# A convolution with a routed feed-forward network: a later group's placing put behind the first slot's turn, fewer parts ahead, and three more groups convolved by parts

## Chip, cores and metric

The kernel runs on one core of one Trainium2 chip. The metric is the device time of one execution in microseconds, taken as the median of several runs. Profiles come from one further execution, recorded by the hardware profiler. Engine names are those of the profile: PE is TensorE (PEld its weight loads), DVE is VectorE, ACT is ScalarE, POOL is GpSimd, and SP is SyncE, which here only issues DMAs (its queue is SPq).

## The reference

Two stages. First a causal depthwise convolution over the sequence: 8 sequences of 3584 tokens with 192 channels, 7 taps per head, 8 heads of 24 channels, the taps of a head made by a softmax. Then a top-1 routed network on the 28672 tokens that come out:

```python
w = softmax(weight)                                   # (8 heads, 7 taps)
x = causal_conv(x, w).reshape(28672, 192)             # float32
logits = x @ w_gate + modality_bias[modality_id]      # (28672, 8)
e_idx = argmax(logits, 1); gate = softmax(logits)[e_idx]
out[t] = gate[t] * (relu(x[t] @ w1[e]) @ w2[e])       # e = e_idx[t]; w1 192x1024, w2 1024x192
```

Everything is float32 in and out.

## The kernel before, in words

**Groups.** The convolution and the routing work on 19 groups of tokens (`QUADS_OF_GROUP`, 1, 1, 2, 2, 2 and then 4 quads each; a quad is four tiles of 112 tokens). A group is loaded (`load`, L246), convolved head by head on PE (`convolve`, L266) into a PSUM bank of 8 heads in turn, and copied from there into a buffer `y` in SBUF by ACT for two heads of three and by DVE for the third (L281, L283). There are four `y` buffers; a group of four quads takes two of them, and writes them again only when the scatters of the group that had them have landed. Then come, quad by quad, a transposition on DVE (`turn`, L300), a split for the gate (`part_turned`, L303), the gate's product on PE (`gate`, L320), the logits (L327), and for the whole group `choose` (L334, softmax and argmax on DVE, an exponential on ACT) and `place` (L364, the row of each token in its expert's list, on DVE, from two small PE products). `send` scatters the rows to DRAM by indirect DMAs on POOL (L212).

**Two ways to convolve.** Groups below `WHOLE_X` keep x as float32 in one tile and need one float32 matmul per head with the float32 band (the trace shows it as two MATMUL instructions). The others split x into a rounded half `xh` (ACT, L100) and the remainder `xl` (DVE, L101), quad by quad in `part` (L257), and take three matmuls in the reduced format F32R per head. Their quads are loaded into a ring of three buffers, `xr_0` to `xr_2`, so the fourth quad's load waits for the split of the first. The float32 band lies in the buffer of `xr_0` (L157) as long as a group below `WHOLE_X` is still to be convolved.

**Slots.** The network runs in slots: one expert, 512 rows (chunk 0) or 1024 rows, read back from the scattered lists. Ten chunks of groups feed the slots; chunk 0 is groups 0 to 4 and feeds four slots of two passes of 256 rows. A slot loads w1 and w2 (L623 to L628) and splits them into halves (`split`, L666), brings its rows by DMA (`bring`, L634: `near`, `far`, `tags`), and turns them pass by pass (`turn`, L676: two DVE transpositions, ACT casts, DVE remainders). A pass has four steps: `first` (ten matmuls into `hps`, a ReLU on ACT to `hh`, its remainder `hl` on DVE) and, two steps later, `second` (eight matmuls into two banks `po`), and at the pass's end `put` (an ACT and a DVE operation for each bank, then a scatter to the output).

**Order.** The program is written as generators. `all_groups` (L449) yields after each small part of a group's work; `advance` (L769) runs the next part. `through("groups", 0)` runs the groups of chunk 0; it ends just behind the first head of group 5. Then `start(0)` (L885) brings slot 0, runs `AHEAD` more parts, and writes slot 0's turn. With `AHEAD` 26 these are the rest of group 5, its choice included, and heads 0 and 1 of group 6. After that `run` (L837) writes step by step, and `due` (L795) says how many parts are to have been written by each step: a straight line between marks, the first at `head + AHEAD`. A compiler pass then orders each engine's instructions from its own estimate of when they become ready, so that later work can move ahead of earlier work, with one exception: the ACT instructions written inside `run` keep the order in which they are written (`manual_schedule`, L902). `tc.issue_after(ins)` puts an instruction behind `ins` on the engine of `ins`. All engines execute their queue in order.

Of the kernel before, what the change touches and what calls it, by code (L numbers as in the profile page):

```python
# [14 lines left out]
ALU = mybir.AluOpType  # L15
AX = mybir.AxisListType
PSUM = bass.MemoryType.PSUM

P = 128
MB = 112  # L20
HALO = 16
QUADS_OF_GROUP = (1, 1, 2, 2, 2) + (4,) * 14
WHOLE_X = 10
WHOLE_Y = 5
HEAD_BANKS = dict(turn=1, logit=2, place=2)
ORDERED = {mybir.EngineType.Activation}
# [2 lines left out]
WAIT = 3  # L29
OUTS = 4  # L30
PIN = 18
AHEAD = 26
T = 256
GROUPS_OF_CHUNK = (5, 2, 2, 2, 2, 2, 2, 2, 0, 0)
SLOTS_OF_CHUNK = (4, 3, 3, 4, 3, 4, 3, 3, 3)
# [8 lines left out]
def conv_then_routed_ffn(ctx, tc, x, weight, modality, w_gate, mod_bias, w1, w2, out):  # L44
    nc = tc.nc
    NB, S, D = x.shape
# [8 lines left out]
    NF = FF // P  # L55
    NJ = T // P
# [54 lines left out]
    def warm(n):  # L111
# [9 lines left out]
        out=tri, in_=ones, compare_op=ALU.is_gt, fill=0.0, base=0,  # L121
# [10 lines left out]
    carry = const.tile([MB, E], F32, name="carry0")  # L132
# [91 lines left out]
    class Group:  # L224
# [109 lines left out]
        def choose(self):  # L334

            n = self.tiles
            lg = self.lg

            def per_tile(ap):
                return ap.unsqueeze(2).broadcast_to([MB, n, E])  # L340

            top = rt.tile([MB, NT], F32, name="top")[:, 0:n]
            nc.vector.tensor_reduce(out=top, in_=lg, axis=AX.X, op=ALU.max)
            ex = rt.tile([MB, NT, E], F32, name="ex", bufs=1)[:, 0:n]
            nc.vector.tensor_tensor(out=ex, in0=lg, in1=per_tile(top), op=ALU.subtract)
            nc.scalar.activation(out=ex, in_=ex, func=AF.Exp)
            self.oh = rt.tile([MB, NT, E], BF16, name="oh")[:, 0:n]
            rk = rt.tile([MB, NT, E], F32, name="rk", bufs=1)[:, 0:n]
            nc.vector.tensor_tensor(out=rk, in0=lg, in1=per_tile(top), op=ALU.is_equal)
            nc.vector.tensor_tensor(out=rk, in0=rk, in1=ramp.unsqueeze(1).broadcast_to([MB, n, E]), op=ALU.mult)  # L350
            first = rt.tile([MB, NT], F32, name="first")[:, 0:n]
            nc.vector.tensor_reduce(out=first, in_=rk, axis=AX.X, op=ALU.max)
            nc.vector.tensor_tensor(out=self.oh, in0=rk, in1=per_tile(first), op=ALU.is_equal)
            den = rt.tile([MB, NT], F32, name="den")[:, 0:n]
            nc.vector.tensor_reduce(out=den, in_=ex, axis=AX.X, op=ALU.add)
            nc.vector.tensor_scalar(out=den, in0=den, scalar1=1e-9, scalar2=None, op0=ALU.add)
            for i, y in enumerate(self.ys):
                nc.vector.reciprocal(out=y[0:MB, 0:self.nb, 0], in_=den[:, i * self.nb:(i + 1) * self.nb])
                with tc.issue_after(state["scatter"]) if "scatter" in state else nullcontext():
                    nc.gpsimd.iota(y.bitcast(I32)[0:MB, 0:self.nb, 1], pattern=[[S, self.nb]],  # L360
                                   base=self.b0 * S + (self.block + i) * MB + MB - 1,
                                   channel_multiplier=-1)

        def place(self):  # L364

            n = self.tiles
            oh = self.oh
            rp = self.bank("place", [MB, 2, n, E], F32, "rp")
            ohf = oh.rearrange("p t e -> p (t e)")
            nc.tensor.matmul(rp[:, 0].rearrange("p t e -> p (t e)"), tri, ohf, start=True, stop=True)  # L370
            nc.tensor.matmul(rp[:, 1].rearrange("p t e -> p (t e)"), ones, ohf, start=True, stop=True)
            ad = rt.tile([MB, E * NT], F32, name="ad", tag="ex", bufs=1)[:, 0:E * n].rearrange("p (e t) -> p e t", e=E)
            nc.vector.tensor_copy(out=ad[:, :, 0], in_=state["carry"])
            nc.vector.tensor_copy(out=ad[:, :, 1:n], in_=rp[:, 1, 0:n - 1, :].rearrange("p t e -> p e t"))
            base = rt.tile([MB, E * NT], F32, name="base", bufs=1)[:, 0:E * n].rearrange("p (e t) -> p e t", e=E)
            nc.vector.tensor_tensor_scan(
                out=base.rearrange("p e t -> p (e t)"), data0=keep[n].rearrange("p e t -> p (e t)"),
                data1=ad.rearrange("p e t -> p (e t)"), initial=0.0, op0=ALU.mult, op1=ALU.add)
            after = rt.tile([MB, E], F32, name="carry", bufs=4)
            nc.vector.tensor_tensor(out=after, in0=rp[:, 1, n - 1, :], in1=base[:, :, n - 1], op=ALU.add)  # L380
            pos = rt.tile([MB, NT, E], F32, name="pos", tag="rk", bufs=1)[:, 0:n]
            nc.vector.tensor_tensor(out=pos, in0=rp[:, 0], in1=base.rearrange("p e t -> p t e"), op=ALU.add)
            nc.vector.tensor_tensor(out=pos, in0=pos, in1=oh, op=ALU.mult)
            row = rt.tile([MB, NT], F32, name="row")[:, 0:n]
            nc.vector.tensor_reduce(out=row, in_=pos, axis=AX.X, op=ALU.add)
            self.idx = rt.tile([MB, NT], I32, name="idx", bufs=6)[:, 0:n]
            nc.vector.tensor_copy(out=self.idx, in_=row)
            state["carry"] = after
            state["placed"] += 1
            if state["placed"] == sum(GROUPS_OF_CHUNK[:self.chunk + 1]):  # L390
                state["end", self.chunk] = after
# [19 lines left out]

    def body(cur, after):

        if after:
            for q in range(min(3, after.quads)):
                after.load(q)
        for h in range(H):
            cur.convolve(h)
            yield
        cur.bias_of()  # L420
        gates = []
        ready, step_of = [], 1 if cur.whole_y else 2
        for t in range(cur.quads + 2):
            if t < cur.quads:
                cur.turn(t)
                yield
            if t == 0 and after and after.whole_x and after.quads > 3:
                after.load(3)
            if ready and ready[0][1] < t:
                t0, _, terms = ready.pop(0)  # L430
                gates.append((t0, cur.gate(terms)))
            yield
            if t < cur.quads:
                terms = cur.part_turned(t)
                if (t + 1) % step_of == 0 or t + 1 == cur.quads:
                    ready.append((4 * (t // step_of * step_of), t, terms))
            yield
            while gates:
                cur.logits(*gates.pop(0))
        cur.choose()  # L440
        yield
        if after and not after.whole_x:
            for q in range(after.quads):
                after.part(q)
                if q == 0 and after.quads > 3:
                    after.load(3)
                yield
# [33 lines left out]
    state, tables = {}, {}  # L481
# [129 lines left out]
    class Slot:  # L611


        def __init__(self, i, chunk, ent):
            self.i, self.h, self.passes, self.rows, self.ends, self.tags = i, {}, plan[chunk][2] // T, {}, {}, {}
            self.chunk, self.ent, load = chunk, ent, nc.sync
            with tc.issue_after(state["load"]) if "load" in state else nullcontext():
                e = load.value_load(ent[:, 1:2], min_val=0, max_val=E - 1)
                new = load.value_load(ent[:, 2:3], min_val=0, max_val=1)
            w1e = w1[bass.ds(e, 1), :, :].rearrange("e p n -> (e p) n")  # L620
            w2e = w2[bass.ds(e, 1), :, :].rearrange("e (c p) d -> p (e c) d", p=P)
            only = dict(cond=new, cond_hint=False)
            load.dma_start(out=raw1[i % 2][:, 0, :], in_=w1e[0:P, :], **only)  # L623
            for r in range(2):
                state["load"] = load.dma_start(out=raw1[i % 2][r * DB:(r + 1) * DB, 1, :], in_=w1e[P:D, :], **only).ins
# [50 lines left out]
        def turn(self, k):  # L676
            lot, k0 = divmod(k, LOT)
            tp = ring(sp, 2, [P, NJ + 1, P], F32, "tp")
            with tc.issue_after(state["o"]) if "o" in state else nullcontext():
                nc.vector.transpose(out=tp[:, 0:NJ].rearrange("p j (s t) -> p (j s) t", t=Q),  # L680
                                    in_=self.rows[lot][:, k0 * T // Q:(k0 + 1) * T // Q])
# [8 lines left out]
            for hi, lo, raw in pieces:  # L690
                turned = nc.vector.tensor_tensor(out=lo, in0=raw, in1=f(hi), op=ALU.subtract).ins  # L691
            self.h["x", k] = [z.rearrange("p j s -> p (j s)") for z in (xh, xl, xs)]
            self.h["tag", k] = self.tags[lot][:, k0 * NJ:(k0 + 1) * NJ]
            state["vector"] = turned

        def first(self, k, fp):
            wa = w1b[self.i % 2]
# [13 lines left out]
        def second(self, k, fp):  # L711
            wb = w2b[self.i % 2]
            hh, hl = self.h.pop((k, fp))
            if fp == 0:
                self.po = [ring(ps_g2, 2, [P, 2 * D], F32, "po") for _ in range(NJ)]
            for u in range(2):
                c = 2 * fp + u
                for j, po in enumerate(self.po):
                    js = slice(j * P, (j + 1) * P)

                    def by_hi():
                        nc.tensor.matmul(po, hh[:, u, js], wb[:, c, :], start=c == 0, stop=c == NF - 1,  # L722
                                         skip_group_check=True)

                    def by_lo():
                        nc.tensor.matmul(po[:, 0:D], hl[:, u, js], wb[:, c, 0:D], start=False, stop=False,  # L726
                                         skip_group_check=True)

                    for product in (by_lo, by_hi) if c == NF - 1 else (by_hi, by_lo):
                        product()  # L730
            if fp == NF // 2 - 1:
                self.put(self.h.pop(("tag", k)))

# [201 lines left out]
```

## Time and profile before

| | |
|---|---|
| median of 3 runs | 1276.77 us (1275.79 to 1277.69) |
| the profiled execution | 1274.14 us, its span 1272.4 us |
| PE busy in the span | 1221.3 us (96%) |
| DVE, ACT, POOL busy | 1001.7, 736.9, 519.2 us |
| granted TensorE clock, mean | 0.987 |

A row of the timeline gives the start in us from the span's start, the duration, the engine, the line of the code, the operation, what is written and read, a count of merged instructions, and in brackets the idle time of the engine just before and what ended it. A row of a table by windows gives for each engine the busy time in that stretch and the number of instructions, then the granted TensorE clock as a share, the DMA share and GB/s. A row of the waits gives the total, the number and the longest. A row of the chain of work gives start, duration and what the last-ending chain passed through. Groups of instructions show busy time and the mean ns of one, then idle time before them.

### The profile page before, as it was taken

The page shows a single profiled execution, that of the slowest core. Times are in us where ns is not written, and L with a number is a line of the kernel's source. Part 1 is how long each engine was busy: PE and PEld are TensorE (multiplying, and loading weights), DVE is VectorE, ACT ScalarE, POOL GpSimd, SP SyncE. Part 2 cuts the span into 40 slices and gives each one's busy share as a digit, 9 for nine tenths or more (in the row PEclk, how much of TensorE's full clock was granted, in tenths as well). Part 3 has the DMA queues.
Part 4 walks back from the last instruction along what each step waited for, and adds up shares of the span by engine and source line. Part 5 has one row for each costly group of instructions (what it writes and reads, how often), then busy time and mean ns, then how long its engine had stood idle before and what let it go on. Part 6 is the DMA issues. An engine that isn't in the chain of part 4 may idle for free.

```text
span 1272.4 us, 28546 instructions
## 1 busy us (share of the span) xinstructions
PE 1221.3 (96%) x9106; PEld 1187.7 (93%) x9106; DVE 1001.7 (79%) x2545; ACT 736.9 (58%) x1644; POOL 519.2 (41%) x574
## 2 busy tenths in 40 slices
PE   8559999999999999999999999999999999999996
PEld 6438899999999999999999999999999999999996
DVE  6559988887888778877888788877876676687895
ACT  2226565566666556656665666556555555566774
POOL 5745763625353532624454442613526122121221
PEclk9869999999999999999999999999999999999999
DMA  6567475435453445424355445424424135494440
GB/s 180 158 164 174 125 196 106 108 83 134 100 145 79 98 95 120 133 44 111 63 133 147 110 103 119 114 56 103 101 48 132 37 77 109 104 248 105 91 101 18
DMA packets 314836, 142.24 MB, mean 112 GB/s; under 512 B 229042, under 2 KB 301355, under 8 KB 314676
## 3 DMA queue, kind: packets, MB, share of 16 engines
q1 hardware_dynamic: 289060, 94.97, 35.4%
q0 software_dynamic: 23232, 44.30, 11.0%
q8 instruction: 73, 1.20, 0.4%
q10 hardware_dynamic: 2384, 1.06, 0.3%
q14 instruction: 87, 0.71, 0.2%
HBM read 118.16 MB, written 51.82 MB: 134 GB/s over the span
## 4 chain that ended last, share of the span: by engine, by line
PE 77%; DVE 7%; issue 4%; DMA 4%; POOL 3%; SPq 2%; ACT 2%; DVEq 0%; POOLq 0%; ACTq 0%
PE hps L704 36%; PE po L722 23%; PE po L726 11%; PE cv L276 5%; PE gt L320 3%; POOL routed_rows L212 2%; DVE hl L708 2%; SPq L653 2%; DVE w1b L101 1%; DMA raw<-in_moe_w_dram 1%; DMA routed_rows<-y,idx 1%; DVE w2b L101 1%; DMA near<-routed_rows 1%; ACT lowp L738 0%; DVE sxs L691 0%
## 5 line engine op out<-in xcount | busy, mean ns | idle before, releaser
L722 PE MATMUL po<-w2b,hh 128*128 128x384 f32 x1824 | 556.2, 355 | 3.6 <-DVE o L740 3.4
L704 PE MATMUL hps<-sxh,w1b 128*128 128x256 f32 x1824 | 484.7, 288 | 2.7 <-DVE hl L708 1.3
L741 POOL DMA_INDIRECT out_dram<-o,tags x228 | 233.6, 1024 | 555.8 <-DVE o L740 492.2
L707 ACT ACTIVATE hh<-hps 128x512 fp32r<-128x512 f32 x456 | 273.1, 599 | 314.4 <-PE hps L704 309.1
L708 DVE SCALAR_TENSOR_TENSOR hl<-hps,hh 128x512 fp32r<-128x512 f32 x456 | 311.2, 685 | 178.0 <-ACT hh L707 175.5
L726 PE MATMUL po<-w2b,hl 128*128 128x192 f32 x1824 | 442.6, 253 | 0.0
L704 PE MATMUL hps<-sxs,w1b 128*128 128x256 f32 x1824 | 363.3, 281 | 0.5 <-DVE sxs L691 0.5
L704 PEld LDWEIGHTS hps<-sxh,w1b 128*128 128x128 f32 x1824 | 343.9, 189 | 12.7 <-DVE hl L708 7.9
L722 PEld LDWEIGHTS po<-w2b,hh 128*128 128x128 f32 x1824 | 344.1, 189 | 5.4 <-DVE o L740 4.8
L726 PEld LDWEIGHTS po<-w2b,hl 128*128 128x128 f32 x1824 | 345.7, 190 | 0.0
L212 POOL DMA_INDIRECT routed_rows<-y,idx x256 | 253.7, 991 | 145.4 <-issue 114.2
L704 PEld LDWEIGHTS hps<-sxs,w1b 128*128 128x128 f32 x1824 | 279.6, 189 | 0.9 <-DVE sxs L691 0.7
L704 PE MATMUL hps<-sxl,w1b 128*128 128x256 f32 x912 | 256.1, 281 | 0.6 <-DVE sxl L691 0.6
L704 PEld LDWEIGHTS hps<-sxl,w1b 128*128 128x128 f32 x912 | 172.5, 189 | 3.2 <-DVE sxl L691 0.8
L101 DVE TENSOR_TENSOR w1b<-raw,w1b 128x512 fp32r<-128x512 f32 x152 | 101.1, 675 | 6.6 <-ACT w1b L100 6.1
L738 ACT ACTIVATE lowp<-po,tags 128x192 f32<-128x192 f32 x228 | 83.7, 418 | 31.8 <-PE po L722 31.3
L281 ACT COPY y<-cv 112x192 f32<-112x192 f32 (+1 forms) x198 | 53.4, 319 | 75.5 <-PE cv L276 54.6
L100 ACT CAST w1b<-raw 128x512 fp32r<-128x512 f32 x152 | 92.4, 620 | 0.8
L101 DVE TENSOR_TENSOR w2b<-raw,w2b 128x384 fp32r<-128x384 f32 x152 | 80.9, 542 | 10.3 <-ACT w2b L100 10.0
L740 DVE SCALAR_TENSOR_TENSOR o<-po,tags,lowp 128x192 f32<-128x192 f32 x228 | 84.9, 411 | 4.8 <-ACT lowp L738 2.5
L689 ACT CAST sxs<-tp 64x128 fp32r<-64x128 f32 x228 | 67.9, 298 | 32.6 <-DVE tp L682 29.8
L100 ACT CAST w2b<-raw 128x384 fp32r<-128x384 f32 x152 | 76.1, 512 | 1.0
(133 smaller groups left out, 1032.0 us busy)
## 6 DMA issues: line engine op xcount, KB each, us to landing
raw<-in_moe_w_dram SPq DMA_DIRECT2D x38, 768.0 KB
raw<-in_moe_w_dram SPq DMA_DIRECT2D x38, 512.0 KB
raw<-in_moe_w_dram SPq DMA_DIRECT2D x76, 256.0 KB
xr<-in_x_dram SPq DMA_DIRECT2D x36, 384.0 KB
near<-routed_rows SPq DMA_DIRECT2D x212, 64.0 KB
x<-in_x_dram SPq DMA_DIRECT2D x26, 384.0 KB
far<-routed_rows SPq DMA_DIRECT2D x456, 16.0 KB
routed_rows<-filler SPq DMA_DIRECT2D x8, 776.0 KB
```

The source lines that it names most:

```text
L100: nc.scalar.copy(out=hi, in_=raw)
L101: return nc.vector.tensor_tensor(out=lo, in0=raw, in1=f(hi), op=ALU.subtract).ins
L212: state["scatter"] = nc.gpsimd.indirect_dma_start(out=scr, out_offset=bass.IndirectOffsetOnAxis(ap=idx, axis=0), in_=src, in_offset=None,).ins
L689: nc.scalar.copy(out=hi, in_=raw)
L704: nc.tensor.matmul(hps[:, u, :], wa[:, c, fs], mv[z], start=n == 0, stop=n == len(terms) - 1)
L707: nc.scalar.activation(out=hh, in_=hps, func=AF.Relu)
L708: turn_behind(nc.vector.scalar_tensor_tensor(out=hl, in0=hps, scalar=0.0, in1=f(hh), op0=ALU.max, op1=ALU.subtract))
L722: nc.tensor.matmul(po, hh[:, u, js], wb[:, c, :], start=c == 0, stop=c == NF - 1, skip_group_check=True)
L726: nc.tensor.matmul(po[:, 0:D], hl[:, u, js], wb[:, c, 0:D], start=False, stop=False, skip_group_check=True)
L738: nc.scalar.activation(out=lowp, in_=po[:, D:2 * D], func=AF.Copy, scale=gate)
L740: turn_behind(nc.vector.scalar_tensor_tensor(out=o, in0=po[:, 0:D], scalar=gate, in1=lowp, op0=ALU.mult, op1=ALU.add))
L741: st = nc.gpsimd.indirect_dma_start(out=out, out_offset=bass.IndirectOffsetOnAxis(ap=tag.bitcast(I32)[:, j, 1:2], axis=0), in_=o, in_offse ...
```

## The change

Seven edits, all in the program's text:

1. `WHOLE_X` 10 to 7: groups 7, 8 and 9 are convolved by parts. `parts_of` then counts four more parts for each of groups 6, 7 and 8, at whose end the next group is split.
2. `AHEAD` 26 to 24: heads 0 and 1 of group 6 are no longer written before slot 0's turn, but in `run`.
3. `state["first"]` is the last DVE instruction of slot 0's turn. `choose` puts its first DVE instruction behind it, and so does `place`, where that turn has been written already: the placing of group 5 and everything of later groups.
4. `band_free` in `body`: where the next group is the first by parts (now group 7), its quads are loaded after the current group's eight heads, not before.
5. The weight loads of slots 0 and 1 are no longer conditional.
6. `second`: in a pass's last step the four pairs of matmuls go by bank (both for the first bank, then both for the second) and not in alternation.
7. The marks of `due` move with the counts of parts.

```diff
-WHOLE_X = 10
+WHOLE_X = 7
-AHEAD = 26
+AHEAD = 24
...
 def choose(self):
...
-            nc.vector.tensor_reduce(out=top, in_=lg, axis=AX.X, op=ALU.max)
+            with tc.issue_after(state["first"]) if "first" in state else nullcontext():
+                nc.vector.tensor_reduce(out=top, in_=lg, axis=AX.X, op=ALU.max)
...
 def place(self):
...
-            nc.vector.tensor_copy(out=ad[:, :, 0], in_=state["carry"])
+            with tc.issue_after(state["first"]) if "first" in state else nullcontext():
+                nc.vector.tensor_copy(out=ad[:, :, 0], in_=state["carry"])
...
 def body(cur, after):
-        if after:
+        band_free = after and cur.whole_x and not after.whole_x
+        if after and not band_free:
             for q in range(min(3, after.quads)):
                 after.load(q)
         for h in range(H):
             cur.convolve(h)
             yield
+        if band_free:
+            for q in range(min(3, after.quads)):
+                after.load(q)
...
 class Slot: __init__
-            only = dict(cond=new, cond_hint=False)
+            only = dict(cond=new, cond_hint=False) if i > 1 else {}
...
 class Slot: turn
             state["vector"] = turned
+            state.setdefault("first", turned)
...
 class Slot: second
-            for u in range(2):
-                c = 2 * fp + u
-                for j, po in enumerate(self.po):
-                    js = slice(j * P, (j + 1) * P)
+            at = [(u, j) for u in range(2) for j in range(NJ)]
+            if fp == NF // 2 - 1:
+                at = sorted(at, key=lambda uj: uj[1])
+            for u, j in at:
+                c, po = 2 * fp + u, self.po[j]
+                js = slice(j * P, (j + 1) * P)
...
```

The products themselves (`by_hi`, `by_lo`) and their order within a pair are unchanged.

More of the change, by code (lines that the diff above doesn't have):

```diff
@@ L715, in second, with by_hi, by_lo @@
                 self.po = [ring(ps_g2, 2, [P, 2 * D], F32, "po") for _ in range(NJ)]
-            for u in range(2):
-                c = 2 * fp + u
-                for j, po in enumerate(self.po):
-                    js = slice(j * P, (j + 1) * P)
[L721 to L730, printed above, removed]
+            at = [(u, j) for u in range(2) for j in range(NJ)]
[4 more added lines that the diff above has]
+                js = slice(j * P, (j + 1) * P)
+                def by_hi():
+                    nc.tensor.matmul(po, hh[:, u, js], wb[:, c, :], start=c == 0, stop=c == NF - 1,
+                                     skip_group_check=True)
+                def by_lo():
+                    nc.tensor.matmul(po[:, 0:D], hl[:, u, js], wb[:, c, 0:D], start=False, stop=False,
+                                     skip_group_check=True)
+                for product in (by_lo, by_hi) if c == NF - 1 else (by_hi, by_lo):
+                    product()
             if fp == NF // 2 - 1:
```

## The prediction

> **What bounds the kernel now.** I read the page first, then busy time by windows, then who PE waited for, then the timeline of the opening. The page gives the frame:
>
> ```profile
> span 1272.4 us, 28546 instructions
> PE 1221.3 (96%) x9106; PEld 1187.7 (93%) x9106; DVE 1001.7 (79%) x2545; ACT 736.9 (58%) x1644; POOL 519.2 (41%) x574
> ```
>
> PE is idle for 51.1 us in all (1272.4 - 1221.3). The windows say where, and how DVE stands there:
>
> ```profile
> 60.00:80.00 20.00, 7.73 (x25) 5.55 (x26) 7.27 (x32) 5.55 (x11) 9.06 (x14) 0.57 0.43 106
> 80.00:100.00 20.00, 13.39 (x73) 9.65 (x72) 15.78 (x47) 7.53 (x23) 11.24 (x11) 0.91 0.89 230
> 110.00:120.00 10.00, 8.68 (x67) 8.24 (x66) 9.77 (x22) 6.43 (x13) 3.53 (x7) 1.00 0.63 124
> 120.00:130.00 10.00, 9.13 (x60) 7.76 (x59) 8.70 (x29) 6.04 (x18) 2.07 (x3) 1.00 0.89 222
> 130.00:140.00 10.00, 10.00 (x67) 8.86 (x67) 8.86 (x28) 6.45 (x18) 6.87 (x7) 1.00 0.78 216
> 140.00:150.00 10.00, 8.61 (x65) 7.95 (x64) 9.96 (x30) 5.78 (x12) 8.07 (x7) 1.00 0.22 65
> 150.00:160.00 10.00, 8.69 (x66) 8.25 (x66) 9.77 (x32) 5.16 (x11) 8.32 (x9) 1.00 0.37 114
> 400.00:500.00 100.00, 99.85 (x766) 99.32 (x765) 80.80 (x183) 61.35 (x134) 35.91 (x41) 1.00 0.44 100
> ```
>
> Three stages. From 60 to 100 us PE is idle for 18.9 of 40 us: the passage from the convolution's head to the first slot. From 110 to 160 us DVE is the fuller engine (47.06 of 50 us against PE's 45.11). From 400 us PE is 99.85% busy, so there only work taken from PE counts. What PE waited for:
>
> ```profile
> PE cv L276 <- ACT y L281: 14.4, 4, 6.9
> PE gt L320 <- ACT gx L100: 8.8, 3, 5.9
> PE po L722 <- DVE o L740: 3.4, 5, 0.9
> ```
>
> The opening, from the timeline:
>
> ```profile
> 61.94 0.54 ACT L281 COPY y<-cv 112x192 f32<-112x192 f32 x2 [3.84 <-DMA routed_rows<-y,idx]
> 62.37 0.84 ACT L100 CAST gx<-turned 128x768 fp32r<-128x768 f32 x1
> 75.78 0.54 ACT L281 COPY y<-cv 112x192 f32<-112x192 f32 x2 [7.16 <-DMA routed_rows<-y,idx]
> 75.88 1.96 SPq L653 DMA_DIRECT2D near<-routed_rows  x4
> 76.15 2.90 PE L276 MATMUL cv<-x,band 128*112 128x384 f32 x4 [6.90 <-ACT y L281]
> 78.03 4.39 SPq L653 DMA_DIRECT2D far<-routed_rows  x8
> 78.27 2.27 PE L320 MATMUL gt<-gx,wg_parts 128*128 128x256 f32 x11
> 80.58 0.45 DVE L327 STREAM_TRANSPOSE lt<-gt 128x256 f32<-128x256 f32 x1 [9.66 <-PE gt L320]
> 83.29 0.39 SPq L628 DMA_DIRECT2D raw<-in_moe_w_dram  x1
> 85.79 0.16 DVE L373 COPY ad<-carry 112x8 f32<-112x8 f32 x1
> 88.50 0.17 DVE L387 CAST idx<-row 112x16 int32<-112x16 f32 x1
> 88.68 0.45 DVE L680 STREAM_TRANSPOSE tp<-near 128x256 f32<-128x256 f32 x1
> 90.57 0.30 DVE L682 STREAM_TRANSPOSE tp<-far 128x128 f32<-128x128 f32 x1
> 91.90 0.50 PE L704 MATMUL hps<-sxs,w1b 128*128 128x256 f32 x2 [0.45 <-DVE sxs L691]
> 93.65 1.76 ACT L100 CAST w2b<-raw 128x384 fp32r<-128x384 f32 x4
> 95.73 0.61 ACT L707 ACTIVATE hh<-hps 128x512 fp32r<-128x512 f32 x1
> ```
>
> Read it from the end. The second ReLU (95.73) follows the splits of w2 (93.65), they follow the first ReLU, and that the products from 91.90. Those came late because DVE turned the rows at 88.68, directly behind group 5's choice and placing (85.79 to 88.67 is the placing). Choice and placing were late because group 5's logits (80.58) came late: PE had four convolution matmuls of group 6 ahead of the gate's products, and these waited for PSUM banks that ACT's copies of heads 0 and 1 of group 6 were to free (61.94 and 75.78). Those copies waited, 3.84 and 7.16 us long, for scatters that still read the `y` buffers. The same copies held up group 5's own cast (62.37).
>
> **The change, part by part.** *Fewer parts ahead.* Heads 0 and 1 of group 6 now belong to the part in which ACT keeps the written order, behind the first ReLU. So the four copies leave the opening: group 5's cast and gate no longer stand behind them, and with the gate, logits and choice come before the rows of slot 0 arrive. *Placing behind the turn.* The 2.88 us (85.79 to 88.67) go behind slot 0's turn. What queues behind the delayed placing on DVE: the first remainder `hl`; and behind its result, group 5's sixteen scatters on POOL, for which nobody waits before chunk 1's slots. The cover is the wait for w2 that follows; without it this would cost up to 2.9 us.
>
> What is late next in the opening is data, worked out with landings from the chain of work (the convolution rows serve further down; the x6 row is from the chain's stretch of 288 to 304 us):
>
> ```profile
> 1.65 4.70 DMA x<-in_x_dram
> 103.87 1.48 DMA far<-routed_rows
> 161.21 1.29 PE cv L276 x4
> 290.45 1.04 PE cv L276 x6
> 405.80 2.68 DMA near<-routed_rows
> 1233.00 4.05 DMA raw<-in_moe_w_dram
> ```
>
> `near`: the last issue ends at 77.84, landed 80.5 (+2.68). `far` for the first pass is the first four of eight issues, to 80.2, landed 81.7 (+1.48). From the turn of `far` to the products that need it took 1.33 us (90.57 to 91.90). So these products could run at 83.0 instead of 91.90, if DVE is free. But then w2 is late: issued until 83.68, landed 87.7 at the earliest (+4.05). ACT then splits it (1.76), makes the four copies of heads 0 and 1, now in its way (2 x 0.54), and comes to the second ReLU at 90.5 instead of 95.73: 5.2 us earlier. I take off 1 us, since w2's 768 KB are the larger of the weight loads, and 1.3 us for two convolutions of group 6 that PE did in idle time and now does behind the slot's start (x4 in 1.29 us is two of them). Opening: **-2.9 us**, bounds 0 (the passage is late by something else) and -5.2.
>
> The clock speaks against part of this. After 6.90 us of idling the x4 convolutions at 76.15 took 2.90 us; warm they took 1.29 (161.21). The first slot's products now come after a longer pause, so they will start at that slower rate. I set 0 for it: they lie between 83 and 88 us, where ACT waits for w2 anyway. The Trainium skill, page "TensorE: Matmul & The Clock Gate", Part 1, says that after a window of about 3.4 us without work the array gets half its clock, until about 3.4 us of work have passed; by that rule, without my cover, some 1.7 us (an estimate from that page) would be added and the sum below be -2.5. The rate of the two rows agrees with it.
>
> *Groups 7 to 9 by parts.* Taken from PE: 24 convolutions at 0.645 us (1.29 / 2) become three matmuls each at 0.52 (1.04 / 2). **-3.0 us**, in full only where PE is the bound; bounds 0 and -3.0. Added, per quad:
>
> ```profile
> L101 DVE TENSOR_TENSOR xl<-xr,xh 128x768 fp32r<-128x768 f32 x36 | 33.9, 941 | 0.2
> L100 ACT CAST xh<-xr 128x768 fp32r<-128x768 f32 x36 | 29.8, 829 | 0.7 <-DMA xr<-in_x_dram 0.5
> ```
>
> and, in the timeline, group 10's first and last cast:
>
> ```profile
> 281.20 0.83 ACT L100 CAST xh<-xr 128x768 fp32r<-128x768 f32 x1
> 287.56 0.82 ACT L100 CAST xh<-xr 128x768 fp32r<-128x768 f32 x1
> ```
>
> Twelve quads: 11.3 us on DVE, 9.9 on ACT. ACT has room (6 of 10 us busy in the windows). For DVE it depends on the place. Group 9's quads and group 8's last fall where DVE has a fifth to spare, as at 400 us: 0. Group 7's split (3.8 us) follows group 6's choice, in the full stretch from 110 to 160 us, which has 2.9 us of DVE to spare (50 - 47.06). Between 0 (all of it fits) and 3.8 (nothing does) I take **+2.2**, nearer to the upper end, because the windows with room are not those beside the full ones; for group 8 the same bounds, and 0.
>
> *Halves in turn.* The first bank is finished one pair of matmuls earlier.
>
> ```profile
> L722 PE MATMUL po<-w2b,hh 128*128 128x384 f32 x1824 | 556.2, 355 | 3.6 <-DVE o L740 3.4
> ```
>
> A pair is about 0.3 us of PE (556.2 / 1824; its small partner mostly overlaps). PE waited five times, 3.4 us together, for `o`. At 0.3 us each at most 1.5; nothing at least. I take **-0.5**.
>
> *Later loads, unconditional weights, moved marks.* Group 7's loads leave SP's queue behind w2, so slot 1's weights go out sooner; PE did not wait for them: 0. Without the condition SP issues slot 0's w1 some tenths sooner, but ACT took it up at 76 us behind its own wait, and rows set the opening: 0. The first mark lies 21 steps ahead (32 steps of chunk 0 less `LEAD`), with groups 5 to 7 written by then: 25 + 29 + 29 - 24 = 59 parts, before 75 - 26 = 49. Group 6's placing stays at about step 11 (32 parts at that rate, before 26): 0.
>
> Sum: -2.9 - 3.0 + 2.2 - 0.5 = **-4.2 us**. On the profiled execution's 1274.14 us this gives 1269.9; the median of the runs lies 2.6 us above that execution, so I put 1276.77 - 4.2 = **1272.6 us**. About 0.2% (2.55 us) is what a measurement of this kernel can tell from no change.
>
> **Rivals.** *The vector engine overflows (slower).* At 59 parts in 21 steps (2.81 a step) the splits of groups 7 and 8 are pressed together. The rows at 281.20 and 287.56 show four casts spread over 6.4 us where 54 parts were due in 48 steps (1.13); at the new rate they come within 6.4 x 1.13 / 2.81 = 2.6 us. The fourth quad's load can only go after the first remainder (0.94) and needs some 4.7 us to land (first row of the chain), 5.6 together. ACT keeps its order, so it stands for up to 3.0 us per group, and the ReLUs behind it. With 7.6 us of remainders without room and one such wait, and without the gain of the convolutions of groups 7 and 8: -2.9 - 1.0 - 0.5 + 7.6 + 3.0 = +6.2, **1283.0 us**. For it: 9.96 and 9.77 of 10 us. Against: from 120 to 140 us DVE has 2.4 us left. It turns the forecast to slower once the two groups cost more than 2.2 + 4.2 + 2.55 = 9.0 us together.
>
> *The opening stays (no change).* The compiler's own order may put other DVE work ahead of the turn (group 6's head copies that wait for the same scatters), or w2 and the moved convolutions eat the 5.2 us. Then -3.0 + 2.2 - 0.5 = -1.3, **1275.5 us**. For it: before, that order put the placing ahead of the turn although it was written behind. Against: the copies on ACT do go.
>
> *All of it counts (faster still).* The opening gives 5.2 and the splits find room: -5.2 - 3.0 - 0.5 = -8.7, **1268.1 us**.
>
> **How the numbers follow.** Forecast 0.48, opening stays 0.24, overflow 0.18, all counts 0.10. The forecast's own range is 1269 to 1275 (the opening within 1.1 us of its value, group 7's split between 0 and 3.8); about a tenth of it reaches over the line of -2.55. So faster 0.10 + 0.46 = 0.56, same 0.24 + 0.02 = 0.26, slower 0.18. The range from 1266.5 to 1280 leaves out the upper half of the overflow and little at the lower end.
>
> **What would show it.** In the changed profile: no ACT copy at 62 and 76 us that waits for scatters; group 5's logits before 75 us; the turn of `near` at 80 to 82 us and the placing behind it; the ReLU of the second step at 90 to 92 us; 48 L276 matmuls on the float32 band of 128x384 fewer and 72 by parts more; PE's wait for `o` under 3 us. I am wrong if the turn comes after 86 us, if ACT or SP waits over 2 us for an `xr` load between 110 and 180 us, or if PE's idle time there grows by more than 5 us.

## The result, and the profile after

The changed kernel takes **1292.25 us** (median; 1291.94 to 1292.46), the kernel before took 1276.28 beside it: ratio 1.0124, 95% interval 1.0106 to 1.0142. It is slower, and outside the range. The profiled execution took 1291.94 us.

The experiments ran on four chips. On one (f1, f3, e7, e8) the kernel before took 1276.65 us. On the other three, each called a chip B below, all kernels stood every 70 to 100 us and the granted clock then fell to half for some 17 us (see the last section); the kernel before took 1519 to 1523 us there, and only ratios and single waits are read from these chips.

The page of the kernel after, its span and busy times:

```profile
span 1290.2 us, 28602 instructions
PE 1229.1 (95%) x9130; PEld 1200.6 (93%) x9130; DVE 1008.3 (78%) x2557; ACT 753.9 (58%) x1656; POOL 520.8 (40%) x574
```

The span grew by 17.8 us: PE is idle for 61.1 us in place of 51.1, and busy for 7.8 us more, though its convolutions became cheaper. The windows of the kernel after (stretch, length, then PE, PEld, DVE, ACT, POOL with their counts, granted clock, DMA share, GB/s):

```profile
110.00:120.00 10.00, 8.45 (x53) 8.25 (x54) 8.06 (x24) 3.97 (x9) 2.51 (x4) 0.83 0.71 172
120.00:130.00 10.00, 7.21 (x54) 6.57 (x52) 8.61 (x28) 4.26 (x9) 2.92 (x3) 1.00 0.76 145
130.00:140.00 10.00, 6.22 (x29) 5.57 (x30) 4.07 (x8) 5.13 (x15) 7.80 (x8) 0.83 0.72 217
140.00:150.00 10.00, 9.47 (x70) 9.03 (x68) 9.81 (x24) 7.80 (x18) 8.00 (x10) 1.00 0.25 71
150.00:160.00 10.00, 7.35 (x55) 6.89 (x56) 9.86 (x29) 5.94 (x12) 5.58 (x5) 1.00 0.12 39
160.00:170.00 10.00, 7.76 (x61) 7.51 (x59) 9.29 (x32) 4.11 (x7) 2.01 (x3) 1.00 0.55 139
170.00:180.00 10.00, 3.51 (x13) 3.44 (x14) 3.03 (x6) 3.33 (x9) 0.90 (x1) 0.53 0.71 137
400.00:500.00 100.00, 99.94 (x771) 99.66 (x770) 81.29 (x185) 59.97 (x130) 41.59 (x46) 1.00 0.38 87
```

From 110 to 160 us PE is busy for 38.70 us (before: 45.11), and DVE for 40.41 (before: 47.06). PE lost 6.4 us there, while the engine that was to overflow had *more* room: between 130 and 140 us PE, DVE and ACT all stand for a third of the time or more (POOL is busy for 7.80 us, with scatters), and between 170 and 180 us every engine stands for most of it. Those two windows show a granted clock of 0.83 and 0.53, and the one from 110 to 120 us shows 0.83 as well. The steady stage is as before. Who PE waited for, in the kernel after (total us, times, longest):

```profile
PE cv L276 <- ACT xh L100: 14.1, 2, 8.7
PE cv L276 <- ACT y L281: 6.6, 2, 6.1
...
PE po L731 <- DVE o L749: 5.8, 5, 2.1
```

The first row is new: two waits, 14.1 us, for the cast of an input quad. The wait for `y` fell from 14.4 to 6.6 us: that is the opening, and the forecast's gain. The timeline of the kernel after, with the opening first and then the two stalls:

```profile
71.55 0.45 DVE L327 STREAM_TRANSPOSE lt<-gt 128x256 f32<-128x256 f32 x1 [2.41 <-PE gt L320]
81.49 0.45 DVE L686 STREAM_TRANSPOSE tp<-near 128x256 f32<-128x256 f32 x1 [2.72 <-DMA near<-routed_rows]
84.64 0.17 DVE L375 COPY ad<-carry 112x8 f32<-112x8 f32 x1
89.18 1.76 ACT L100 CAST w2b<-raw 128x384 fp32r<-128x384 f32 x4 [2.01 <-DMA raw<-in_moe_w_dram]
91.68 0.62 ACT L714 ACTIVATE hh<-hps 128x512 fp32r<-128x512 f32 x1
...
110.68 0.39 PE L320 MATMUL gt<-gx,wg_parts 128*128 128x256 f32 x1 [2.48 <-ACT gx L100]
...
118.44 4.89 SPq L659 DMA_DIRECT2D near<-routed_rows  x4
120.04 2.29 ACT L100 CAST xh<-xr 128x768 fp32r<-128x768 f32 x3
121.08 2.66 DVE L101 TENSOR_TENSOR xl<-xr,xh 128x768 fp32r<-128x768 f32 x3
123.51 4.33 SPq L659 DMA_DIRECT2D far<-routed_rows  x8
128.03 0.39 SPq L659 DMA_DIRECT2D tags<-routed_rows  x1
128.52 6.47 SPq L254 DMA_DIRECT2D xr<-in_x_dram  x4
132.77 0.83 ACT L100 CAST xh<-xr 128x768 fp32r<-128x768 f32 x1 [8.47 <-DMA xr<-in_x_dram]
133.66 1.30 PE L276 MATMUL cv<-xh,band_hi 128*112 128x384 f32 x3 [5.33 <-ACT xh L100]
136.70 0.60 ACT L714 ACTIVATE hh<-hps 128x512 fp32r<-128x512 f32 x1
...
164.42 1.26 SPq L631 DMA_DIRECT2D raw<-in_moe_w_dram  x2
164.98 0.94 DVE L101 TENSOR_TENSOR xl<-xr,xh 128x768 fp32r<-128x768 f32 x1
166.02 0.39 SPq L634 DMA_DIRECT2D raw<-in_moe_w_dram  x1
167.92 0.43 SPq L254 DMA_DIRECT2D xr<-in_x_dram  x1
175.61 0.83 ACT L100 CAST xh<-xr 128x768 fp32r<-128x768 f32 x1 [8.56 <-DMA xr<-in_x_dram]
176.49 0.98 PE L276 MATMUL cv<-xh,band_hi 128*112 128x384 f32 x2 [8.73 <-ACT xh L100]
```

*The opening* went by the forecast's steps: logits at 71.55, turn at 81.49 as the rows land, placing behind it at 84.64, then w2 as the late thing. The second ReLU starts at 91.68 in place of 95.73.

*Group 7.* Three quads have buffers. The first remainder frees one at about 122.0 (121.08 + 2.66 / 3). But SP issues in order, and its next 13 DMAs are a slot's rows and tags (from 118.44 to 128.42). The load goes out at 128.52 (the row counts the next group's first three loads with it), 6.5 us late, and ACT can use it 4.2 us later. ACT has stood for 8.47 us. Since it runs in a written order, the ReLU behind the cast waits too, and with it the slot's products: nothing is left for PE.

*Group 8.* Here the buffer is free at 165.92 and the load goes out at 167.92, so the queue costs 2 us; but ACT can use it only after 7.7 us; it goes directly behind a slot's weights. ACT stands for 8.56 us, PE for 8.73, and PE then starts at half clock.

The start of each ReLU is a ruler along the kernel: one per step, 456 in all, counted from 0. Before, and the differences from before, in us:

| ReLU | 1 | 10 | 13 | 20 | 21 | 33 | 38 | 80 | 455 |
|---|---|---|---|---|---|---|---|---|---|
| before | 95.73 | 124.55 | 134.02 | 157.82 | 160.16 | 193.34 | 207.97 | 319.39 | 1259.10 |
| after | -4.05 | -0.84 | +6.47 | +7.92 | +16.60 | +16.56 | +19.07 | +18.37 | +17.79 |
| f1, groups 7 to 9 in float32 | -5.49 | -4.88 | -4.97 | -2.05 | -2.05 | -2.04 | -2.00 | -2.14 | -2.44 |
| f3, fourth buffer | -3.98 | -0.76 | -1.03 | +0.82 | +0.85 | +0.96 | +0.83 | -0.70 | -3.32 |
| e7, load from GpSimd | -6.30 | -3.07 | +1.62 | +2.65 | +12.54 | +13.75 | +13.69 | +12.10 | +11.52 |
| e8, group 9 alone by parts | -4.86 | -4.27 | -4.36 | -1.45 | -1.45 | -1.51 | -1.57 | -3.20 | -3.41 |

The loss comes in three steps: 7.3 us between ReLU 10 and 13, 8.7 between 20 and 21, 2.5 between 33 and 38. Another 3.2 us of the opening's gain go between ReLU 1 and 10, in f3 and e7 too; they are taken up further down. For the third step, the timeline of the kernel after:

```profile
205.03 0.94 POOL L212 DMA_INDIRECT routed_rows<-y,idx  x1 [0.30 <-DMA routed_rows<-y,idx]
206.28 1.12 POOL L750 DMA_INDIRECT out_dram<-o,tags  x1 [0.30 <-DVE hl L715]
215.51 0.42 DVE L749 SCALAR_TENSOR_TENSOR o<-po,tags,lowp 128x192 f32<-128x192 f32 x1 [3.79 <-DMA out_dram<-o,tags]
```

POOL issues group 7's scatters (L212) ahead of the output's (L750), one every 1.25 us; DVE then waits 3.79 us for an `o` buffer that the output scatter still reads, and PE 2.13 us for DVE. That the delays brought these together is argued, not tried; in e7, where group 8 was late as well, this step is missing.

### The profile page after: what moved, and what is told of

Same layout as the page of the kernel before. It is cut to its first block, busy times and chain, and to the rows that moved or that the text cites. A ratio compares the mean times of both kernels' runs of the same rounds, so it can differ in the third digit from the quotient of the medians.

```text
span 1290.2 us, 28602 instructions
## 1 busy us (share of the span) xinstructions
PE 1229.1 (95%) x9130; PEld 1200.6 (93%) x9130; DVE 1008.3 (78%) x2557; ACT 753.9 (58%) x1656; POOL 520.8 (40%) x574
## 3 DMA queue, kind: packets, MB, share of 16 engines
q10 hardware_dynamic: 2384, 1.06, 0.3%
## 4 chain that ended last, share of the span: by engine, by line
PE 76%; DVE 9%; DMA 5%; issue 4%; SPq 2%; POOL 2%; ACT 2%; DVEq 0%; POOLq 0%; ACTq 0%
PE hps L711 35%; PE po L731 22%; PE po L735 10%; PE cv L276 5%; PE gt L320 3%; DMA routed_rows<-y,idx 2%; DVE hl L715 2%; POOL routed_rows L212 2%; SPq L659 1%; DMA out_dram<-o,tags 1%; PE hps L115 1%; ACT hh L714 1%; DVE w2b L101 1%; DVE w1b L101 1%; DMA near<-routed_rows 1%
## 5 line engine op out<-in xcount | busy, mean ns | idle before, releaser
L750 POOL DMA_INDIRECT out_dram<-o,tags x228 | 236.1, 1035 | 571.7 <-DVE o L749 512.7
L735 PE MATMUL po<-w2b,hl 128*128 128x192 f32 x1824 | 427.2, 255 | 0.0
L731 PEld LDWEIGHTS po<-w2b,hh 128*128 128x128 f32 x1824 | 336.0, 189 | 7.7 <-DVE o L749 6.9
L212 POOL DMA_INDIRECT routed_rows<-y,idx x256 | 254.9, 996 | 155.9 <-issue 118.1
L747 ACT ACTIVATE lowp<-po,tags 128x192 f32<-128x192 f32 x228 | 95.9, 421 | 19.3 <-PE po L731 13.4
L749 DVE SCALAR_TENSOR_TENSOR o<-po,tags,lowp 128x192 f32<-128x192 f32 x228 | 88.2, 411 | 11.0 <-DMA out_dram<-o,tags 7.9
```

Of the source, the lines that this page charges most:

```text
L212: state["scatter"] = nc.gpsimd.indirect_dma_start(out=scr, out_offset=bass.IndirectOffsetOnAxis(ap=idx, axis=0), in_=src, in_offset=None,).ins
L747: nc.scalar.activation(out=lowp, in_=po[:, D:2 * D], func=AF.Copy, scale=gate)
L749: turn_behind(nc.vector.scalar_tensor_tensor(out=o, in0=po[:, 0:D], scalar=gate, in1=lowp, op0=ALU.mult, op1=ALU.add))
L750: st = nc.gpsimd.indirect_dma_start(out=out, out_offset=bass.IndirectOffsetOnAxis(ap=tag.bitcast(I32)[:, j, 1:2], axis=0), in_=o, in_offse ...
```

## The experiments

Theory A: the fourth quad's load is late, and ACT, in its written order, holds the ReLUs behind it. Theory B, the prediction's own slower case in its main part: the twelve splits don't fit on DVE.

**Groups 7 to 9 again in float32** (f1; e1 on a chip B). All else of the change stays.

```
-WHOLE_X = 7
+WHOLE_X = 10
```

> The changed kernel with groups 7 to 9 again convolved whole in float32, all else of the change kept. Both theories: the opening's gain of some 3 to 4 us shows at the second ReLU, part of it is eaten in the full stretch of the vector engine up to 125 us, and no cast waits for an xr load: ratio to before 0.997 to 0.9995. If it is at or above 1.001, the order edits cost something by themselves and the splitting is not the whole cause.

> The changed kernel with WHOLE_X back at 10, so groups 7 to 9 keep their float32 convolution; all other edits stay. Theory A (the loss is ACT standing for the fourth quad's load of groups 7 and 8): the two idle times of PE of 5.33 and 8.73 us and the slow clock behind them are gone, the opening keeps the 4.05 us that it gained by the second ReLU, of which the full DVE between 100 and 120 us may take up to 3.2 again: 1272 to 1276 us. Theory B (the order edits cost something later that the comparison hides behind the stalls): 1278 us or more.

f1: 1271.63 us, ratio 0.9963 (0.9950 to 0.9975). e1: 0.9974 (0.9956 to 0.9991). What is left of the change is a gain; the whole loss hangs on the parts.

**The parts without the order edits** (e2, on a chip B): the kernel before with `WHOLE_X = 7` and the later loads that go with it.

```
-WHOLE_X = 10
+WHOLE_X = 7
...
+        band_free = after and cur.whole_x and not after.whole_x
+        if after and not band_free:
```

> The kernel before with groups 7 to 9 by parts and the later loads that go with it, nothing else. Theory A: the stalls belong to the parts and not to the opening, so they come here too, about as long: PE idle 5 us and 8 us or more for ACT's fourth cast of groups 7 and 8, 1276.3 + 18 + 3 = 1293 to 1299 us. Theory B (the earlier opening or the changed pace of the parts makes the loads late): at most half of it, 1278 to 1286 us.

Ratio 1.0097 (1.0067 to 1.0126), between the two cases expected. Group 8's fourth cast of e2 in the timeline:

```profile
206.74 0.83 ACT L100 CAST xh<-xr 128x768 fp32r<-128x768 f32 x1 [8.40 <-DMA xr<-in_x_dram]
```

The same wait, with AHEAD at 26 and the placing where it was: it belongs to the parts. Group 7's was 1.23 us here, where its load met a gap in SP's queue.

**A fourth buffer** (f3; e3 on a chip B): four `xr` buffers, all four quads loaded together. Three constants of the opening moved into buffers not yet in use, to make room. All splits are done.

```
-ring(xp, 3, [P, 4, D], F32, "xr")
+ring(xp, 4, [P, 4, D], F32, "xr")
...
-                if q == 0 and after.quads > 3:
-                    after.load(3)
```

> The changed kernel with a fourth xr buffer, all four quads of a group loaded together. Theory A (the fourth load is late, stands behind another slot's loads in SP's queue, and ACT waits for it in its order): the two waits of 8.5 us and the stretches of half clock behind them are gone, though the split work is all there; ratio 0.997 to 1.002, within 2 us of the float32 groups. Theory B (12 splits have no room on the vector engine in the full stretch): the gap to the float32 groups stays at 8 us or more, ratio 1.006 to 1.012.

> The changed kernel with a fourth buffer in the ring of quads, so that the fourth quad's load waits for no split of the same group and is issued with the other three. Room is made by laying the identity and the gate's small weight tiles into buffers that are used later; computed is the same. Theory A (it is the late load): no ACT cast of a quad waits over 2 us, PE's two long idle times go, 1271 to 1276 us. Theory B (the 12 splits themselves fill DVE and ACT in the full stretch): the time stays above 1284 us and PE waits there for DVE instead.

f3: **1270.59 us**, ratio 0.9958 (0.9944 to 0.9972); e3: 0.9990 (0.9972 to 1.0008). The timeline and the windows of f3:

```profile
120.12 2.29 ACT L100 CAST xh<-xr 128x768 fp32r<-128x768 f32 x3
124.41 0.83 ACT L100 CAST xh<-xr 128x768 fp32r<-128x768 f32 x1
```

```profile
120.00:130.00 10.00, 9.65 (x66) 8.61 (x66) 9.73 (x24) 7.42 (x18) 1.98 (x2) 1.00 0.73 146
130.00:140.00 10.00, 9.43 (x69) 9.18 (x68) 9.68 (x29) 8.12 (x22) 6.99 (x7) 1.00 0.73 211
```

The fourth cast no longer stands, DVE does fill up (9.73 and 9.68 of 10), and yet PE has 9.65 and 9.43 where it had 7.21 and 6.22. Theory A holds. What the splits cost by themselves is small beside it (further down). By the ruler the late loads cost 18.37 + 0.70 = 19.1 us at ReLU 80, and all three steps are gone, the third with the others.

**The fourth load from GpSimd** (e7), for groups 7 and 8, so that it isn't behind SP's slot.

```
+            by = nc.gpsimd if q == 3 and not self.whole_x and self.chunk <= 2 else nc.sync
...
-                nc.sync.dma_start(out=xr, ...
+                by.dma_start(out=xr, ...
```

> The changed kernel with three buffers as it stands, but the fourth quad's load of groups 7 and 8 issued by GpSimd instead of SyncE, so that it does not stand behind a slot's rows and weights in SP's queue; GpSimd has the output's scatters ahead of it instead. Theory A with the queue as the cause: the first wait (8.5 us, group 7) falls under 3 us and the second is shorter by what the weights in front of it took; ratio 1.003 to 1.008. If the buffer coming free or the transfer itself is the cause, and not the queue: the waits and the ratio stay within 0.002 of the changed kernel's 1.0124. Theory B: the same, no change.

1286.35 us, ratio 1.0081 (1.0063 to 1.0099). Its timeline:

```profile
120.63 0.83 POOL L255 DMA_DIRECT2D xr<-in_x_dram  x1
126.34 0.83 ACT L100 CAST xh<-xr 128x768 fp32r<-128x768 f32 x1 [4.26 <-DMA xr<-in_x_dram]
164.90 0.83 POOL L255 DMA_DIRECT2D xr<-in_x_dram  x1
171.54 0.83 ACT L100 CAST xh<-xr 128x768 fp32r<-128x768 f32 x1 [9.76 <-DMA xr<-in_x_dram]
```

Group 7's load went out 7.9 us sooner, of which 2.2 us are this run's earlier start (its first cast is at 117.81 us, in place of 120.04), and its wait halved, to 4.26 us; not under 3, since the load alone took 5.7 (120.63 to 126.34). Group 8's did not shrink: POOL had two output scatters and two operations of its own ahead, so the load went out 4.3 us after its buffer was free, and the transfer (6.6 us) went behind the weights as before. So the queue is the main cause for group 7. For group 8 it is the transfer behind the weights, by comparison only: such a load took 7.5 us in e2, again behind weights, and 3.4 us in g1 (below), where the last weights had gone out 9.5 us before. In both groups the load's start hangs on the first remainder.

**Fewer groups by parts** (e8: group 9 alone; g1 on a chip B: groups 8 and 9): `WHOLE_X = 9` and `WHOLE_X = 8`.

> The changed kernel with group 9 alone by parts, 7 and 8 in float32. Theory A: the changed kernel showed no wait for group 9's fourth load, so its 8 convolutions give their 1.0 us and nothing is taken: ratio 0.001 below the float32 groups, 0.996 to 0.999. Theory B: group 9 lies where the vector engine has room, so the same. If its fourth load now waits over 3 us, the wait depends on the pace of the groups before it, and the ratio is 1.002 to 1.006.

> The changed kernel with group 7 in float32 and groups 8 and 9 by parts. Group 9 alone stood at ratio 0.9946, the changed kernel at 1.0124, so 22.8 us lie between them for groups 7 and 8. If each of the two waits brings its own loss (some 8 us of idle array, the half clock, the scatters bunched behind it), one of them is left: ratio 1.001 to 1.005, a wait of 4 to 9 us at group 8's fourth cast and none at group 7's. If group 8's wait was only drawn in by group 7's delay, it is gone: ratio 0.994 to 0.997. If the wait simply moves to the first group by parts, the ratio stays over 1.006.

e8: **1269.51 us**, ratio 0.9946 (0.9931 to 0.9962). No cast waits for a load, and e8 is 1.06 us ahead of f1 at ReLU 80, from 0.5 us behind it at ReLU 33: the gain of eight convolutions. g1: 1.0007 (0.9995 to 1.0019). The timeline of g1 shows the wait without group 7's delay, behind the first `far` rows:

```profile
191.40 0.40 SPq L254 DMA_DIRECT2D xr<-in_x_dram  x1
194.81 0.83 ACT L100 CAST xh<-xr 128x768 fp32r<-128x768 f32 x1 [5.66 <-DMA xr<-in_x_dram]
```

So each of groups 7 and 8 makes its own wait. With one of them g1 stands 0.6% above e8 (1.0007 against 0.9946, on different chips).

**The order edits** on the kernel before, on chips B: both (e4, g2, h1), fewer parts alone (e5, g3, h2), choice and placing behind the turn alone (e6).

```
-AHEAD = 26
+AHEAD = 24
...
+            with tc.issue_after(state["first"]) if "first" in state else nullcontext():
```

> The kernel before with AHEAD 24 and with choice and placing behind the first slot's turn; conditional weight loads, alternating halves and float32 groups 7 to 9 as before. Theory A: this is the whole gain of the opening, second ReLU at 91.7 us, 1272 to 1276 us, within 1 us of the kernel that has the other small edits too. Theory B (the unconditional loads or the halves carry part of it): over 1.5 us slower than that kernel.

> The kernel before with 24 parts ahead and the choice and placing behind the first turn, nothing else. The float32 version of the changed kernel had its second ReLU 5.5 us earlier than before. If these two edits together make the opening, the second ReLU comes 4 to 6 us earlier here too, and the ratio is 0.996 to 0.9985. If the later loads and the unconditional first weights are part of it, it comes under 3 us earlier.

> The kernel before with 24 parts ahead and the choice and placing behind the first turn, once more. If these two make the opening: on a chip without the periodic throttling, the second ReLU 4 to 6 us earlier than before, ratio 0.996 to 0.9985. If the later loads and the unconditional first weights are part of it: under 3 us earlier. On a throttled chip only the ratio can be read.

> The kernel before with 24 parts ahead in place of 26 and nothing else. The forecast put the opening's gain down to the copies of heads 0 and 1 of group 6 leaving ACT's way, with the placing behind the turn as the second half. If the fewer parts do most of it, group 5's logits come some 5 us earlier and the second ReLU 2 to 4 us earlier (93.5 to 91.5 us), ratio 0.997 to 0.9995. If the placing still stands ahead of the turn, the second ReLU moves by under 1 us and the ratio is 0.9995 to 1.0015.

> The kernel before with 24 parts ahead and nothing else. If the opening needs both edits, the placing of group 5 still stands ahead of the first turn, the second ReLU moves by under 2 us, ratio 0.999 to 1.001. If fewer parts are enough by themselves, the second ReLU comes 4 us or more earlier.

> The kernel before with 24 parts ahead alone, once more. If both edits are needed: the second ReLU moves by under 2 us, ratio 0.999 to 1.001, and group 5's placing stands ahead of the first turn. If fewer parts are enough: 4 us or more earlier, ratio as of both together.

> The kernel before with a later group's choice and placing issued behind the first slot's turn, still 26 parts ahead. If the rows wait for the placing alone, the second ReLU comes 2 to 4 us earlier and the ratio is 0.997 to 0.999. If the logits are the late thing (the copies of group 6 that wait for scatters), the turn runs earlier but the products of the gate still stand ahead of the slot on PE: the second ReLU moves by under 1.5 us, ratio 0.9985 to 1.001.

Ratios: both 0.9982, 0.9998, 0.9984; fewer parts alone 1.0004, 0.9976, 0.9997; behind the turn alone 1.0006 (0.9997 to 1.0016). The same kernel's ratios differ by up to 0.0028, as much as their intervals allow (each some 0.0015 to either side), so the times don't tell the edits apart. The traces show the parts that each leaves. First e6, then h2:

```profile
82.40 0.54 ACT L281 COPY y<-cv 112x192 f32<-112x192 f32 x2 [9.11 <-DMA routed_rows<-y,idx]
87.93 0.45 DVE L327 STREAM_TRANSPOSE lt<-gt 128x256 f32<-128x256 f32 x1 [12.38 <-PE gt L320]
```

```profile
88.19 0.17 DVE L373 COPY ad<-carry 112x8 f32<-112x8 f32 x1
91.09 0.45 DVE L680 STREAM_TRANSPOSE tp<-near 128x256 f32<-128x256 f32 x1
```

With 26 ahead the copies still wait for scatters and the logits are late; with 24 ahead alone these waits are gone, but the placing still stands ahead of the turn, by 2.9 us as before. What each is worth stays open.

**The halves alone** (e10, on a chip B).

```
+            if fp == NF // 2 - 1:
+                at = sorted(at, key=lambda uj: uj[1])
```

> The kernel before with the halves of a slot's last step in turn, and nothing else. The forecast gave it 0.5 us, at most 1.5: ratio 0.9985 to 1.000, PE's wait for o under 3.4 us in total, and the profile's last ReLU no more than 1.5 us earlier than before. A rival: finishing one bank first exposes the evacuation of the other, ratio 1.000 to 1.002.

Ratio 0.9993 (0.9981 to 1.0006): no more than can be told from nothing.

**Fourth buffer and group 9 alone** (e9, g4, both on chips B).

> The changed kernel with the fourth xr buffer and group 9 alone by parts. The fourth buffer was 1.1 us faster than the float32 groups though it carried a split of 2.4 us in the full stretch, most of which it gave back after 80 ReLUs; group 9 alone gave 1.0 us. If both add, 2 to 3 us below group 9 alone: 1266.5 to 1268, ratio 0.992 to 0.994. If the late gain came only with groups 7 and 8 by parts, it is as group 9 alone: ratio 0.994 to 0.996.

> The changed kernel with the fourth xr buffer and group 9 alone by parts. If the fourth buffer's late gain (2.6 us between the 80th and the last ReLU) holds without groups 7 and 8 by parts, it beats group 9 alone: 1266.5 to 1268.5, ratio 0.992 to 0.994. If not, 1269 to 1271.

Ratios 0.9944 (0.9931 to 0.9957) and 0.9966 (0.9950 to 0.9982): better than before, no better than e8. f3's gain of 2.6 us between ReLU 80 and 455 is not confirmed as the buffer's. Less waiting it is not: PE is idle for 2.1 us in that stretch both in f3 and in the changed kernel, and the same 7174 matmuls keep it busy for 2.0 us less. Why is open.

## Why the prediction was wrong

**The step that failed** is the price of the fourth quad's load, in the rival "The vector engine overflows": one wait of 3.0 us, in a case given 0.18. The runs showed two, of 8.47 and 8.56 us, and no overflow. The reckoning was remainder (0.94) plus transfer (4.7) less 2.6 us of casts. It left out the issue: SP had a slot's 13 DMAs ahead (6.5 us for group 7). It took the transfer from the kernel's first load, which has nothing ahead of it: behind the weights it was 7.7 us (group 8). And since the load stood in a case about DVE, its chance followed DVE's room; the forecast itself had no term for it. What came in with it: PE, already without other work, began again at half clock. That cost some 3.6 us more, estimated from the windows: 0.83 between 130 and 140 us means 3.4 us at half, of which PE worked all but some 0.6; between 170 and 180 us it worked for 3.51 us at half, and a further 0.9 behind that; half of 2.8 + 4.4 is lost. The third step, 2.5 us, had no place in the forecast at all.

**The opening, -2.9.** Right in its steps, and in size: the second ReLU came 4.05 us earlier in the changed kernel, 4.0 to 6.3 in f1, f3, e7 and e8; f1 keeps 2.1 us of it at ReLU 80. In the changed kernel 3.2 of the 4.05 were gone by ReLU 10, before the fourth load: PE stood 2.48 us for a cast (110.68) and then 0.87 us for a remainder of group 6's gate, and the clock was at half from 112.61 to 116.03 us. The clock at 0 held for the opening: it was at half until 88.72 us, but ACT got w2 only at 89.18.

**Convolutions by parts, -3.0.** The counts are as said: in the grouped lines of the kernel after there are 96 of each of the three products (72 before) and 32 whole ones of this shape (80 before):

```profile
L276 PE MATMUL cv<-xl,band_hi 128*112 128x384 f32 x96 | 33.3, 347 | 0.0
L276 PE MATMUL cv<-x,band 128*112 128x384 f32 x32 | 17.1, 665 | 8.1 <-ACT y L281 6.1 <-DVE y L283 0.9 <-DVE lt L327 0.5
```

Group 9's 1.0 us came out as 1.06 (e8 against f1 at ReLU 80), or 1.6 if e8's later start is taken off.

**Group 7's splits on DVE, +2.2.** Without the late load, f3 stands 1.44 us behind f1 at ReLU 80 with the 3.0 us of convolutions inside: 4.4 us. But it stood 1.51 us behind at ReLU 1, before any of this, so some 2.9 us are left, near the term. The place was wrong: at ReLU 9, before the first cast of group 7 (120.12 us), f3 is already 4.95 us behind f1, and by ReLU 20 only 2.88. So most of the loss comes ahead of the splits. What differs there is that the kernels by parts write group 6's parts faster (59 parts in 21 steps, where f1 has 51 by the same count; the forecast put 0 for it) and the window at half clock; which of them it is was not tried.

**Halves, -0.5.** f1 waits 2.7 us for `o` in place of 3.4, and gains 0.3 us between ReLU 80 and 455: small, as said. Of the changed kernel's 5.8 us, 2.13 are the wait of the third step.

The signs named for being wrong came as named: ACT waited over 2 us for an `xr` load, and PE's idle time from 110 to 180 us grew by 15.1 us (20.0 in place of 4.9). With the fourth buffer the same change comes to 1270.59 us, close to the forecast's 1272.6, but that is in part luck: at ReLU 80 that kernel is only 0.70 us ahead of the one before, and the other 2.6 us come later, from no term of the forecast.

## What to carry to other kernels

Price a load that waits for a buffer from the moment the buffer is free to the moment the data is used: what the issuing engine has queued ahead, what shares the DMA engines, and then the transfer, each from its own row. When an engine keeps a hand-written order, one late operand stops everything written behind it, so such a load needs its own case and its own chance. A busy engine's room says nothing about a wait that empties all engines.

## What the runs showed of the hardware

The clock fell to half after less idling than a whole window. In these traces it changes in steps of 3.41 us. Windows of f3 and of the kernel after (stretch, length, PE busy, clock, DMA share, GB/s):

```profile
147.01:150.42 3.41, 1.56 (x12) 1.00 0.22 69
150.42:153.83 3.41, 3.08 (x14) 0.50 0.10 34
```

```profile
153.57:156.99 3.42, 1.57 (x13) 1.00 0.09 31
156.99:160.40 3.41, 2.72 (x19) 1.00 0.08 29
```

Almost the same idle time, 1.85 us, led to half clock in one and to full in the other. In the six traces that are not from a chip B no full-clock window with under 1.6 us idle was followed by a half one, and none with over 1.9 by a full one. The Trainium skill, page "TensorE: Matmul & The Clock Gate", Part 1, gives a free-running window of 3413 ns, which agrees with these rows, and an idle window as the cause; here about half a window of idling was enough, so a gap of 2 us can cost the 3.4 us behind it at half rate, depending on where it falls.

On the chips B the engines stood first, and the clock followed. In e1, in the steady stage:

```profile
460.00:470.00 10.00, 1.70 (x6) 1.44 (x6) 0.69 (x7) 0.00 (x0) 6.88 (x9) 0.51 0.43 132
463.09 0.37 PE L711 MATMUL hps<-sxs,w1b 128*128 128x256 f32 x1 [1.75 <-issue]
```

From about 457 to 471 us PE's matmuls start some 2 us apart and wait for nothing that the profile shows ("issue"), DVE and ACT hardly run, and the clock goes to half only at 460.3 us. This came every 70 to 100 us, whatever the kernel: PE is idle for 220 us in e1 and for 45 us in f1, the same kernel. No run tells why.
